# Attention, Fourier mixing and a feed-forward layer on one core: block products for all chunks, sums shared with GpSimd, new load order and schedule

## The chip, the cores and the metric

The kernel runs on one core of a Trainium2 chip. The core has engines that work beside each other, each through its own list of instructions in order: TensorE (PE, matrix products; its weight loads are listed apart, as PEld), VectorE (DVE), ScalarE (ACT), GpSimd (POOL) and SyncE (SP, which here only issues transfers). They wait for each other by semaphores. Transfers (DMAs) are issued from the queues of SP, ACT and POOL and run on 16 DMA engines.

The metric is the device time of one execution in microseconds (us); less is better. It is given as the median of several runs. A profiled execution is a run of its own: it has its own time, and its span (from the first to the last recorded instruction) is somewhat shorter than that time.

## The reference

All inputs and the output are float32. Batch B = 4, heads H = 8, sequence S = 768, head size 64, so the model width is 512; n_global = 8, n_local = 96.

```python
# attention: q, k, v (4, 8, 768, 64)
scores = scale * np.matmul(q, k.transpose(0, 1, 3, 2))
rel = pos[:, None] - pos[None, :]
is_global = pos[None, :] < int(n_global)
is_local = (rel >= 0) & (rel < int(n_local))
dist = np.where(is_global & ~is_local, float(n_local), np.abs(rel))
scores = scores - slopes[:, None, None] * dist
scores = np.where(is_global | is_local, scores, -1000000000.0)
a = softmax(scores)
x = np.matmul(a, v)            # heads side by side: (4, 768, 512)
# mixing and feed-forward
mixed = np.real(np.fft.fft(np.fft.fft(x, axis=1), axis=2))
u = x + mixed
un = (u - mean(u)) / np.sqrt(var(u) + 1e-06)
return u + np.maximum(un @ w_ch1, 0.0) @ w_ch2      # w_ch1 (512, 2048), w_ch2 (2048, 512)
```

(`softmax` stands for the three lines of the usual form, with 1e-09 added to the sum.)

## The kernel before

*The stages.* All products run on 16-bit values. For each batch b (0 to 3) there are three kinds of stage, and a fourth and fifth behind them.

- Attention. For each pair of heads, q and k are transposed; in batches 0 and 1 by TensorE (L654, with the identity `ident` as its second operand), in batches 2 and 3 by transposing transfers that SP issues (L633). Scores are then made for the band and the global keys (L731 to L751). The distances come in by a product with a table `misc` (loaded from `distm`, helper `dma_const`, L1610) in batches 0 and 1, and in batches 2 and 3 by a multiplication with masks `mk`, which ScalarE makes from a second table `distk`. ScalarE takes exponentials (L765, L768), TensorE the products with v (`pav`, L824), and VectorE divides by the sums (`norm`, L836), into a buffer X.
- Mixing. The two Fourier transforms are made by folds (sums and differences on VectorE, from `fold_0` and `fold_s`/`fold_d`; batches 1 to 3 get a mirrored copy through DRAM: `xd` is written, `xr` read by SP, and `xg` gathered by GpSimd, L889), then products with tables t1 and t2 (`y_unit`, `u_unit`, L1107 and about), a layer norm (mean, square, `rstd` on GpSimd at L1287, `un` on ScalarE or VectorE at L1271 and L1280), and a transpose of `un` to `unT`, by TensorE (L1311) or by transfer.
- First product. The 3072 rows are cut into 12 *chunks* of 2 x 128 rows, three for each batch. `ph_unit(c, jp)` makes an eighth of `relu(un @ w1)` of chunk c: 8 matmuls of 256 columns (L1341), and an evacuation with the relu on ScalarE (L1346) or VectorE (L1347), into `hT`.
- Second product, with two forms. The first CS = 2 chunks use `pg_unit(c, t, part)` (L1362): for each half t of the rows, four units of four matmuls of 512 columns (L1372), each of which needs one quarter (`part`) of w2, and one evacuation with the residual (L1383). The chunks from CS on use block products: `s_sums(c)` (L1432) makes four sums s1, s2, s4, s3 of blocks of `hT` (each 128 x 1024, VectorE), `w2_sums(i)` (L1417) makes sums of blocks of w2 once, in two halves i, and `pg_units(c)` (L1477) makes seven products of 8 matmuls of 256 columns (L1486) in place of the eight that the plain form amounts to; they are named p1, p45 (two products in one unit), p6, p7 and p32, and their results are evacuated from the banks pgA and pgD (L1504).

*The sums of w2* are made in place: `one` (L1422) reads two quarters and writes into `misc`, when the scores of batch 1 no longer need it; `rest` (L1426 to L1428) makes three more, the first of them over a block of w2 itself.

```python
def one():
    VT(W2T(1)[:, k0], W2[0][:, k1, HC:Dm], W2[0][:, k0, HC:Dm], op=ALU.subtract)
...
pl.later([("DVE", dve2(1024), one)], [("w2", 3), ("w2", 1)] + ..., 0.0, [("w2a", i)], rank=2)
pl.later([("DVE", 3 * dve2(1024), rest)], [("w2a", i), ("pgdone",)] + ..., 0.0, [("w2t", i)], rank=2)
```

`pgdone` says that the chunks below CS have read all of w2 in its first form. (`k0` and `k1` are four of the sixteen row blocks of w2 each; the half i = 0 reads quarters 0 and 2, the half i = 1 quarters 1 and 3. The list given to the planner names two of them only; the instruction itself waits for what it reads.)

*The order.* Nothing of the order on the engines comes from the program's loops. The class `Plan` holds a list for each engine, `ORDER`, written out by hand, and emits the instructions in these orders. The constants for the cost of an operation (`act`, `dve`, `pool`, the figures in the calls of `later`) tell the planner when it believes things happen; they decide in which sequence the heads of the five lists are emitted, and alter no instruction. The names in the lists:

- on PE: A0, A1, ... attention units, M0, ... mixing units, H0, ... first products (H(8c + jp) is eighth jp of chunk c), G0, ... second products;
- on the others: `H6.0` is operation 0 of unit H6 (its evacuation), and T.0, T.1, ... are the operations that belong to no PE unit, numbered as the program makes them. T.0 to T.7 are the loads of q and k of the first pair of heads, and their casts; T.8 is the identity, T.9 the distance table, T.10 the table `back`, T.26 the table t1, T.27 t2, T.35 the table `distk`, T.54 to T.57 the quarters of w1 (`wload`, L1678), T.58 to T.61 v of batch 1, T.62 to T.65 the quarters 0 to 3 of w2 (L1678), T.91 the read `xr` of batch 1. T.93 to T.98 are the fold of batch 1; T.97 is its part g1 and T.98 its part g2. The sums of w2 and of the chunks follow behind; their numbers move with the change: the two halves of `one` and `rest` are T.259 to T.262 before, and T.270 to T.273 after; the sums of the chunks begin at T.201 (chunk 2 before, chunk 0 after).

*Queues.* Most loads (q, k, v, the tables t1 and t2, w1, w2) are cast to 16 bit on their way and are issued by GpSimd one by one (`swq`), among GpSimd's computing work. The first loads (first pair of q and k, the identity, the two distance tables, `back`) and the stores are issued by SP and ACT. At the start ACT's list was `T.2 T.4 T.8 T.3 T.5` (a half of q, a half of k, the identity, two casts) and SP's `T.6 T.0 T.9 T.136 T.35 T.127 ...`: the other halves, the distance table, and, among the transposes of batch 2, `distk`. The read T.91 stood behind six of these transposes.

The functions that the change touches and what calls them:

Of the kernel before, what the change touches and what calls it, by code (L numbers as in the profile page):

```python
# [12 lines left out]
ALU = mybir.AluOpType  # L13
# [11 lines left out]
class Plan:  # L25
# [11 lines left out]
    LAT = {"ACT": 0.14, "DVE": 0.12, "POOL": 0.08}  # L37
# [84 lines left out]
    def op_go(self, eng, name, start):  # L122
# [6 lines left out]
        if eng == "POOL":  # L129
            self.ports.append((start, end, 1 if dma else 0 if outs and outs[0][0] in ("vB", "kB") else 2))  # L130
# [21 lines left out]

    SHARED = {"kB": 1, "vB": 1, "sid": 1, "f1": 0, "f2": 0, "f3": 0, "z": 0, "g0": 0, "w": 0, "s": 0, "w2a": 0, "w2t": 0, "ex": 0}
# [3 lines left out]
    def beside(self, start, cost, kind):  # L157
# [4 lines left out]
        if names:  # L162
            s = self.op_start("POOL", names[-1])
            if s is not None:
                p = self.made[names[-1]]
                ports = ports + [(max(s, start), max(s, start) + p[0]["POOL"][0], 1 if p[7] else 0 if p[3] and p[3][0][0] in ("vB", "kB") else 2)]
# [54 lines left out]
    def unit_start(self, unit):  # L221
# [7 lines left out]
        if not there:  # L229
# [1558 lines left out]
```

## Time and profile before

| | us |
|---|---|
| median of 3 runs | 248.52 (247.92 to 248.96) |
| profiled execution, its own time | 248.1 |
| its span | 246.3 |
| busy in the span: TensorE | 230.6 (94%) |
| VectorE | 193.6 (79%) |
| ScalarE | 138.6 (56%) |
| GpSimd | 114.1 (46%) |

The rows that are shown below come from these views. The page's strip cuts the span into 40 equal slices (6.16 us each) and gives a row for each engine, for the granted TensorE clock, and for the GB/s moved. A table by stretch gives the start and end of a stretch, its length, and then for each engine the busy time in it. The chain of waits goes back from the last instruction and gives start, length and what ran. The timeline gives start, duration, engine, line, operation, and `out<-in` by the names of the tiles, with the shape and the count of equal instructions put together. A group of a line gives the count and min/median/max in ns, and from when to when. The list of transfers gives name, queue, size, and the us from issue to landing. The page's list of groups gives the busy time, the mean in ns of one, and the idle time of that engine just before them with what ended it. In these names `pg` is the bank of the plain second product, `pgA` and `pgD` are those of the block products, `qk<-in_k_dram` is a load of k, `sc` a score bank, `py` that of a y product, and `u` holds the residual and, at the end, the output.

### The profile page before, as it was taken

The page shows a single profiled execution, that of the slowest core. Times are in us where ns is not written, and L with a number is a line of the kernel's source. Part 1 is how long each engine was busy: PE and PEld are TensorE (multiplying, and loading weights), DVE is VectorE, ACT ScalarE, POOL GpSimd, SP SyncE. Part 2 cuts the span into 40 slices and gives each one's busy share as a digit, 9 for nine tenths or more (in the row PEclk, how much of TensorE's full clock was granted, in tenths as well). Part 3 has the DMA queues.
Part 4 walks back from the last instruction along what each step waited for, and adds up shares of the span by engine and source line. Part 5 has one row for each costly group of instructions (what it writes and reads, how often), then busy time and mean ns, then how long its engine had stood idle before and what let it go on. Part 6 is the DMA issues. An engine that isn't in the chain of part 4 may idle for free.

```text
span 246.3 us, 7605 instructions
## 1 busy us (share of the span) xinstructions
PE 230.6 (94%) x3251; PEld 191.2 (78%) x3251; DVE 193.6 (79%) x420; ACT 138.6 (56%) x226; POOL 114.1 (46%) x162
## 2 busy tenths in 40 slices
PE   7497896999999998999999999999999999999994
PEld 2375774788668567888988888898889898888883
DVE  2389995879974669999999699899998756746483
ACT  2289687874747458677447788464443761434200
POOL 8699985978391018999139046700210230011020
PEclk9999999999999999999999999999999999999999
DMA  7999999999999999999999989221380240040212
GB/s 178 171 163 141 157 223 148 201 189 201 125 133 168 211 181 204 111 139 114 220 208 266 136 110 148 50 23 22 133 296 4 43 130 0 0 130 1 89 65 106
DMA packets 96082, 32.89 MB, mean 134 GB/s; under 512 B 84304, under 2 KB 92624, under 8 KB 96048
## 3 DMA queue, kind: packets, MB, share of 16 engines
q0 software_dynamic: 66176, 17.06, 72.7%
q1 hardware_dynamic: 26560, 12.56, 25.8%
q10 hardware_dynamic: 3312, 2.79, 3.9%
q8 instruction: 25, 0.41, 0.7%
q14 instruction: 9, 0.07, 0.1%
HBM read 31.48 MB, written 8.65 MB: 163 GB/s over the span
## 4 chain that ended last, share of the span: by engine, by line
PE 49%; DMA 21%; DVE 15%; ACT 4%; POOL 4%; SPq 3%; issue 2%; ACTq 0%; DVEq 0%; POOLq 0%
PE ph L1341 21%; PE pgD L1486 12%; PE pgA L1486 9%; DMA v<-in_v_dram 6%; DMA t<-t1m 4%; DMA ident<-idm 3%; SPq L633 3%; DMA out_dram<-u 3%; PE pav L824 2%; ACT ex L768 2%; DMA unT<-un 2%; POOL qk L554 2%; DMA xr<-xd 2%; DVE tt L836 2%; DMA qk<-in_q_dram 2%
## 5 line engine op out<-in xcount | busy, mean ns | idle before, releaser
L1341 PE MATMUL ph<-unT,w 128*128 128x256 f16 x768 | 94.4, 273 | 1.4 <-DMA unT<-un 0.7
L1341 PEld LDWEIGHTS <-w 128*128 128x128 f16 x768 | 73.7, 98 | 13.2 <-issue 1.2
L1346 ACT ACTIVATE hT<-ph 128x512 f16<-128x512 f32 x73 | 42.9, 596 | 55.1 <-PE ph L1341 53.1
L1486 PEld LDWEIGHTS <-hT 128*128 128x128 f16 x320 | 31.0, 98 | 4.3 <-issue 0.4
L1287 POOL TENSOR_SCALAR sm<-sm 128x2 f32<-128x2 f32 x12 | 3.5, 291 | 58.7 <-ACT un L1280 58.3
L765 ACT ACTIVATE er<-sc 128x1024 f16<-128x1024 f32 (+1 forms) x24 | 22.3, 951 | 11.6 <-PE sc L739 8.0
L1347 DVE TENSOR_SCALAR hT<-ph 128x512 f16<-128x512 f32 x23 | 15.7, 687 | 12.6 <-PE ph L1341 12.6
L768 ACT ACTIVATE ex<-sc 128x1024 f16<-128x1024 f32 (+1 forms) x24 | 21.6, 955 | 5.7 <-PE sc L745 5.6
L1504 DVE SCALAR_TENSOR_TENSOR u<-pgA,sm,u 128x256 f32<-128x256 f32 (+1 forms) x30 | 16.9, 568 | 5.6 <-PE pgA L1486 5.1
L1504 DVE SCALAR_TENSOR_TENSOR u<-pgD,sm,u 128x512 f32<-128x512 f32 (+1 forms) x21 | 15.1, 720 | 3.2 <-PE pgD L1486 3.0
L1357 POOL DMA_INDIRECT out_dram<-u,back x4 | 4.6, 1146 | 27.8 <-DVE rev L1142 16.3
L889 POOL DMA_INDIRECT xr<-xd,back x3 | 4.6, 1525 | 26.1 <-PE sc L739 16.6
L1120 ACT ACTIVATE zy<-py 128x1024 f16<-128x1024 f32 (+1 forms) x13 | 11.1, 857 | 8.8 <-PE py L1107 6.1
L1372 PE MATMUL pg<-w,hT 128*128 128x512 f16 x64 | 16.0, 380 | 0.0
L780 DVE TENSOR_TENSOR ex<-er,mk 128x1024 f16<-128x1024 f16 (+1 forms) x24 | 15.1, 645 | 0.7 <-ACT er L765 0.7
L1280 ACT ACTIVATE un<-un 128x512 f16<-128x512 f16 x24 | 15.0, 625 | 1.1 <-DMA unT<-un 1.1
L1271 ACT ACTIVATE un<-u,sm 128x512 f16<-128x512 f32 x19 | 13.1, 717 | 2.4 <-DVE sm L1238 1.0
L554 POOL DMA_DIRECT2D qk<-in_k_dram x16 | 13.7, 901 | 1.1 <-DMA w<-in_moe_w_ch_dram 0.7
L824 PEld LDWEIGHTS <-ex 128*128 128x128 f16 x352 | 12.6, 97 | 2.0 <-issue 1.2
L824 PE MATMUL pav<-v,ex 128*128 128x65 f16 x224 | 13.1, 193 | 0.6 <-DVE x L836 0.5
L554 POOL DMA_DIRECT2D qk<-in_q_dram x16 | 13.6, 868 | 0.0
L836 DVE TENSOR_TENSOR x<-pav,rc 128x384 f16<-128x384 f32 x24 | 12.6, 554 | 0.6
(168 smaller groups left out, 489.3 us busy)
## 6 DMA issues: line engine op xcount, KB each, us to landing
w<-in_moe_w_ch_dram POOLq DMA_DIRECT2D x8, 512.0 KB, 13.5
out_dram<-u SPq DMA_DIRECT2D x15, 256.0 KB, 2.4
v<-in_v_dram POOLq DMA_DIRECT2D x12, 192.0 KB, 7.6
qk<-in_k_dram POOLq DMA_DIRECT2D x16, 96.0 KB, 6.8
qk<-in_q_dram POOLq DMA_DIRECT2D x16, 96.0 KB, 5.3
xr<-xd SPq DMA_DIRECT2D x3, 512.0 KB, 4.7
xd<-x ACTq DMA_DIRECT2D x2, 768.0 KB, 5.6
v<-in_v_dram POOLq DMA_DIRECT2D x8, 96.0 KB, 5.4
```

The source lines that it names most:

```text
L554: nc.gpsimd.dma_start(qk16[n][:, w, :, h], src[b, h0 + h].rearrange("(i m) d -> m i d", m=P))
L765: A(mine(), cut(pa), AF.Exp, 0.0, 0.125)
L768: A(cut(expst[hp][:, :, g * 512:g * 512 + (384 if g == 2 else 512)]), cut(pa), AF.Exp, 0.0, 0.125)
L780: VT(o, mine(), m, op=ALU.mult)
L824: nc.tensor.matmul(o[:, s * 65:(s + 1) * 65], lhsT, w, start=(a == 0), stop=(a == len(ops) - 1), skip_group_check=True)
L836: VT(X[b][:, 3 * (k.start + h):3 * (k.start + h) + 3, 2 * hp * Dh:(2 * hp + 2) * Dh].rearrange("p y (h d) -> p y h d", d=Dh), pv[:, h, :, ...
L1341: nc.tensor.matmul(ph[:, a * CH:(a + 1) * CH].rearrange("p (x m) -> p x m", x=2), W1[0][:, d, jb * P:(jb + 1) * P], UNT[c][:, :, d, :], st ...
L1346: pl.later([("ACT", act(512), lambda: A(dst, ph, AF.Relu)), ("DVE", dve(512), lambda: V.tensor_scalar_max(dst, ph, 0.0))], [], e, [("h", c ...
L1347: ("DVE", dve(512), lambda: V.tensor_scalar_max(dst, ph, 0.0))],
L1372: nc.tensor.matmul(pg, HT[c][:, jb, t * P:(t + 1) * P], W2[0][:, jb, :], start=(jb == 0), stop=(jb == NJ - 1))
L1486: nc.tensor.matmul(o, lhs(j), rhs(j), start=(first and j == 0), stop=(j == NK - 1), skip_group_check=True)
L1504: V.scalar_tensor_tensor(o, x, r(t), acc, op0=ALU.mult, op1=ALU.add)
```

## The change

CS goes from 2 to 0: all 12 chunks use block products. So `pg_unit` is made for no chunk, nothing waits for `pgdone`, `w2_sums` can come before the first second product and has to come before p45 of chunk 0, and the buffer `tt` that was X of batch 1 has only one earlier user (`WTI` is 1; X of batch 1 is now the buffer `x`, which X of batch 0 also uses). For chunks above 2 a sum of `s_sums` may be put on GpSimd; the new order puts twelve there: T.221, T.220 (chunk 3), T.226 (chunk 4), T.229 (chunk 5), T.238, T.236 (chunk 6), T.242 (chunk 7), T.247, T.248 (chunk 8), T.253, T.254 (chunk 9) and T.266 (chunk 11).

The loads at the start: ACT's list becomes `T.8 T.2 T.4 T.9 T.7 T.3 T.5` and a little later `T.35`; SP's becomes `T.6 T.0 T.10 T.91 T.127 ...`. In GpSimd's list the table t1 goes ahead of the w2 quarter that stood before it, and the w2 quarters come in the order 3, 2, 1, 0; the last of them, T.62, stands behind all loads of batches 0 and 1 and behind two small ones of batch 2 (T.110 and T.103).

All five lists are new. On PE, the first products and the mixing around the start of the second products are in another sequence (the first second product, G0, comes after H13 and before H14, M18, H8 and M16; G1 is p45 of chunk 0). On VectorE, T.270 (`one`) stands between T.97 and T.98; the constants of the planner are others.

```diff
-    CS = 2
+    CS = 0
...
+def pool2(n):
+    return 0.2 + n / 450.0
...
-        def s1():
-            VT(new(0), block(1, 0), block(1, 1), op=ALU.add)
...
+        def s1(on=V):
+            on.tensor_tensor(new(0), block(1, 0), block(1, 1), op=ALU.add)
+
+        def s3(on=V):
+            on.tensor_tensor(block(1, 0), block(0, 0), block(1, 0), op=ALU.subtract)
...
         us = dve2(NK * P)
+
+        def slow(fn):
+            return [("POOL", pool2(NK * P), lambda: fn(nc.gpsimd))] if c > 2 else []
...
-        pl.later([("DVE", us, s1)], hs + sfree(0), 0.0, [("s", c, 1)], rank=1)
+        pl.later([("DVE", us, s1)] + slow(s1), hs + sfree(0), 0.0, [("s", c, 1)], rank=1)
...
-        pl.later(ways if soon else ways[:1], needs, 0.0, [tok], lat=1.0 if soon else 3.2, dma=us)
+        pl.later(ways if soon or tok == ("dk",) else ways[:1], needs, 0.0, [tok], lat=1.0 if soon else 3.2, dma=us)
...
         "PE": (
...
-            "A39 A29 M3 M9 A32 M7 A33 A40 M8 M10 A31 M6 A27 M11 M13 A44 H2 H7 A43 H4 H3 M12 A42 H0 H1 A41 H12 G4 H13 H11 G0 H6 H5 M14 G1 G5 G6 H15 G7 H14 "
+            "M3 A38 A32 A33 M7 M9 A27 A28 M8 A29 M6 A44 A31 M11 A43 M10 H2 A41 M13 A42 H0 H7 M12 H3 H1 H6 H9 H10 H5 H12 H15 H11 M15 H4 M19 H13 G0 H14 M18 "
+            "H8 M16 G1 G2 M14 M17 G3 G4 A46 H22 H19 G5 H23 H17 A47 G7 G6 H16 A45 A53 H18 H20 G8 G9 H21 A52 A51 H24 G10 M20 H26 G11 H28 H27 G12 A55 A50 "
...
         "ACT": (
-            "T.2 T.4 T.8 T.3 T.5 A1.2 A3.0 A4.0 A2.0 A8.0 A9.0 A7.0 A20.0 A18.0 A19.0 A13.0 A12.0 A14.0 A30.1 A37.0 A36.0 T.72 M0.0 T.77 M0.1 A25.1 M1.0 "
+            "T.8 T.2 T.4 T.9 T.7 T.3 T.5 A1.1 A3.0 A4.0 T.35 A2.0 A9.0 A7.0 A18.0 A20.0 A19.0 A14.0 A8.0 A13.0 A12.0 A30.1 A34.1 A35.0 T.72 T.77 M0.0 "
...
         "DVE": (
...
+            "A42.0 T.93 T.94 T.95 T.96 M13.2 T.97 T.270 T.98 T.272 T.271 T.201 T.273 M13.4 T.202 G0.0 T.99 G1.0 T.204 G2.0 T.203 M14.0 G3.0 H14.0 G4.0 "
...
         "POOL": (
...
+            "A34.0 T.26 T.60 T.27 T.59 A26.0 T.58 T.55 T.54 T.57 A25.0 T.65 T.87 T.88 T.56 T.85 T.86 T.64 T.84 T.110 T.63 T.103 T.62 T.104 T.105 T.108 "
...
+            "T.152 T.125 T.122 T.153 T.170 T.160 T.166 M17.5 T.164 T.154 T.157 T.163 T.126 T.155 T.156 T.162 T.168 T.221 T.220 M17.11 T.141 M20.5 T.226 "
...
         "SP": (
-            "T.6 T.0 T.9 T.136 T.35 T.127 T.133 T.128 G7.1 T.134 T.91 G3.1 T.10 T.137 T.130 T.100 T.131 T.101 T.102 T.176 T.182 T.177 T.34 T.185 T.183 "
+            "T.6 T.0 T.10 T.91 T.127 T.128 T.206 T.133 T.205 T.130 T.134 T.136 T.131 T.100 T.137 T.101 T.217 T.176 T.177 T.102 T.216 T.182 T.34 T.185 "
```

More of the change, by code (lines that the diff above doesn't have):

```diff
@@ L36 @@
     LANDED = {"HW": 0.55, "SW": 1.3}
-    LAT = {"ACT": 0.14, "DVE": 0.12, "POOL": 0.08}
+    LAT = {"ACT": 0.18, "DVE": 0.12, "POOL": 0.08}
     def __init__(self):
@@ L129, in op_go @@
         if eng == "POOL":
-            self.ports.append((start, end, 1 if dma else 0 if outs and outs[0][0] in ("vB", "kB") else 2))
+            self.ports.append((start, end, 1 if dma else 0 if outs and outs[0][0] in ("vB", "kB", "ts", "w1s", "s") else 2))
         if dma:
@@ L165, in beside @@
                 p = self.made[names[-1]]
-                ports = ports + [(max(s, start), max(s, start) + p[0]["POOL"][0], 1 if p[7] else 0 if p[3] and p[3][0][0] in ("vB", "kB") else 2)]
+                ports = ports + [(max(s, start), max(s, start) + p[0]["POOL"][0], 1 if p[7] else 0 if p[3] and p[3][0][0] in ("vB", "kB", "ts", "w1s", "s") else 2)]
         for a, b, dma in ports:
@@ L854, in part @@
             m = k.stop - k.start
-            pl.later([("DVE", 0.17 + 0.03 * m + m * dve(384), lambda: norm(po, k))], free(*XT[b]), e,
+            pl.later([("DVE", 0.08 + 0.03 * m + m * dve(384), lambda: norm(po, k))], free(*XT[b]), e,
                      [("x", b, hp, z) for z in range(k.start, k.stop)], CD(b, ring), ring=ring, rank=RA(b))
@@ L1274, in centre @@
         for a in range(2):
-            pl.later([("ACT", 0.62, lambda a=a: un("ACT", a)), ("DVE", 1.3 if c < 2 else 0.38, lambda a=a: un("DVE", a))],
+            pl.later([("ACT", 0.62, lambda a=a: un("ACT", a)), ("DVE", 1.3 if c < 2 else 0.55, lambda a=a: un("DVE", a))],
                      [("u", c, a)] + free("un", c), 0.0, [("un", c, a)])
@@ L1288, in rstd @@
             nc.gpsimd.tensor_tensor(r, r, mhalf, op=ALU.pow)
-        pl.later([("POOL", 0.82, rstd)], [("ss", c, 0), ("ss", c, 1)], 0.0, [("rstd", c)], rank=2)
+        pl.later([("POOL", 1.25, rstd)], [("ss", c, 0), ("ss", c, 1)], 0.0, [("rstd", c)], rank=2)
     def nt_dma(c):
```

47 lines of the change are left out of this document (23 added, 24 removed), and 59 rows, old and new, of the table ORDER.

## The prediction

> **What bounds the kernel now.** I read the busy time by stretch first, then the chain of waits, then single rows. Each row below is a stretch, its length, and the busy time (and instruction count) of TensorE (PE), its weight loads, VectorE (DVE), ScalarE (ACT) and GpSimd (POOL); then the granted clock, the DMA share and GB/s.
>
> ```profile
> 8.68:50.00 41.32, 34.94 (x900) 27.98 (x900) 34.21 (x86) 31.30 (x40) 34.73 (x54) 1.00 1.87 172
> ...
> 65.70:100.00 34.30, 33.45 (x374) 23.18 (x364) 25.10 (x55) 21.04 (x35) 16.52 (x20) 1.00 1.26 171
> 100.00:180.00 80.00, 79.46 (x1142) 69.67 (x1140) 74.91 (x154) 50.46 (x86) 39.92 (x52) 1.00 1.06 132
> 180.00:242.74 62.74, 62.70 (x588) 55.88 (x586) 43.31 (x91) 23.51 (x43) 6.39 (x10) 1.00 0.23 72
> 242.74:246.30 3.56, 0.00 (x0) 0.00 (x0) 0.48 (x1) 0.00 (x0) 0.00 (x0) 1.00 0.31 112
> ```
>
> From 65.7 us to 242.74 TensorE is idle for 1.4 us in all, and it works through a hand-written order. So the end is: the time at which some TensorE unit starts, plus the TensorE work behind it, plus a tail of 3.56 us. VectorE is the second bound: 74.91 of 80 us between 100 and 180. Only before 50 us has TensorE slack (6.4 us idle), and there the chain of waits names loads (start, length, what):
>
> ```profile
> 1.82 6.81 DMA ident<-idm
> 8.68 1.32 PE pt L654 x24
> ...
> 27.83 10.04 DMA t<-t1m
> ...
> 38.52 14.24 DMA v<-in_v_dram
> ```
>
> The first transposes wait for the identity, the first y product for the table t1, the last attention of batch 1 for v. At 172 GB/s the loads are one stream that GpSimd's queue feeds.
>
> **The change part by part.**
>
> *Start.* The identity goes from third to first on ScalarE's load queue, the distance table from SyncE's to fourth on ScalarE's.
>
> ```profile
> 1.76 0.48 SPq L1610 DMA_DIRECT2D misc<-distm  x1
> 7.18 0.52 ACT L599 ACTIVATE hT<-u 128x384 f16<-128x384 f32 x1 [2.59 <-DMA u<-in_k_dram]
> ...
> misc<-distm SPq DMA_DIRECT2D x1, 320.0 KB, 6.1
> distk<-distkm SPq DMA_DIRECT2D x1, 160.0 KB, 2.7
> ...
> 10.93 0.41 PE L731 MATMUL sc<-misc 64*64 64x512 f16 x4
> ```
>
> With the identity early, the last of the four casts (7.18 + 0.52 = 7.70) decides: 8.68 - 7.70 = 1.0 us gained. Bounds: 0.5, if that k half, now third, lands one issue (0.5) later; 1.8, if the 320 KB table no longer shares the engines with it. I take 1.0. The table now lands about where the identity did (8.6), still ahead of the first scores (10.9). The other table, distk, moves from SyncE's queue, where the transposes of batch 2 stood around it, into this stretch: 160 KB at 172 GB/s delay the GpSimd stream by 0.9 us.
>
> *Products.* Chunks 0 and 1 were 64 products of 512 columns (four rows below are four units of the order); they become 7 block products of 8 x 256 columns per chunk, as chunks 2 to 11 already are.
>
> ```profile
> 60.01 1.03 PE L1372 MATMUL pg<-w,hT 128*128 128x512 f16 x4
> 60.88 1.91 PE L1341 MATMUL ph<-unT,w 128*128 128x256 f16 x16
> ...
> 65.33 0.45 PE L1311 MATMUL ptu<-ident,un 64*64 64x64 f16 x32
> ...
> 70.92 1.03 PE L1372 MATMUL pg<-w,hT 128*128 128x512 f16 x4
> ...
> 116.81 0.87 PE pgA L1486 x8
> ```
>
> From 60.01 to 60.88 a unit of four costs 0.87 us, so a chunk costs 8 x 0.87 = 6.96; a block product costs 0.87, so 7 x 0.87 = 6.09. TensorE saves 2 x 0.87 = 1.7 us.
>
> *The new wait.* The old units took each quarter of w2 as it landed. The new second unit of chunk 0 (p45) needs all of w2, and then the w2 sums and chunk 0's first sum. When does w2 land? Issue times and times to landing of three w2 loads and the k load behind them:
>
> ```profile
> L1678 POOL DMA_DIRECT2D w<-in_moe_w_ch_dram x1: 759/759/759, 46.0 to 46.0; - x1
> DMA to landing us min/median/max: 13.0/13.0/13.0
> ...
> L1678 POOL DMA_DIRECT2D w<-in_moe_w_ch_dram x1: 742/742/742, 47.6 to 47.6; - x1
> DMA to landing us min/median/max: 13.9/13.9/13.9
> ...
> L554 POOL DMA_DIRECT2D qk<-in_k_dram x1: 822/822/822, 51.6 to 51.6; - x1
> DMA to landing us min/median/max: 13.4/13.4/13.4
> ```
>
> ```profile
> GB/s 178 171 163 141 157 223 148 201 189 201 125 133 168 211 181 204 111 139 114 220 208 266 136 110 148 50 23 22 133 296 4 43 130 0 0 130 1 89 65 106
> ```
>
> Landings at 59.0 and 61.5: 2.5 us each; the last w2 load stands between that and the k load (65.0), so it lands at about 64.0. The new GpSimd order has the same loads ahead of the last w2 load (all of batches 0 and 1, tables, weights, two small ones of batch 2); only their order differs, so 64.0 again, between 62 (the thin fourth and fifth slices of 141 and 157 GB/s below, where GpSimd made copies between its issues, filled up to 172: 2 x 6.16 us x 23 / 172 = 1.6) and 65.5 (distk, new pauses). The last is now T.62, the first quarter, and VectorE's first w2 sum (T.270) reads just that quarter.
>
> VectorE does not get there late: its last norm began at 60.47, and the new order puts A41 to A44 ahead of five first-product units (4.4 us), so about 56 to 55 even with the front as it is; the fold up to the end of g1 took 69.40 - 60.47 = 8.9.
>
> ```profile
> 60.47 1.02 DVE L836 TENSOR_TENSOR tt<-pav,rc 128x384 f16<-128x384 f32 x2
> ...
> 69.40 0.95 DVE L1077 TENSOR_TENSOR eA<-zy 128x1536 f16<-128x1536 f16 x1
> ...
> 71.20 0.74 DVE L1383 SCALAR_TENSOR_TENSOR u<-pg,sm,u 128x512 f32<-128x512 f32 x1
> ...
> 133.32 0.68 DVE L1450 TENSOR_TENSOR eg<-hT 128x1024 f16<-128x1024 f16 x1
> 133.92 0.74 DVE L1504 SCALAR_TENSOR_TENSOR u<-pgD,sm,u 128x512 f32<-128x512 f32 x1
> ```
>
> So T.270 waits at the head of VectorE's queue, at 61 to 64 us, until 64.0. Behind it stand, in order, g2 of batch 1 (71.20 - 69.40 = 1.8), a second sum, three sums, s1 of chunk 0, three sums: nine sums at 133.92 - 133.32 = 0.60 make 5.4. p45 can start at 64.0 + 5.4 + 1.8 = 71.2. TensorE meanwhile has only p1, H14, M18, H8 and M16 (4.1 us) and idles some 3 us. That is where the front's gain goes: t1 is issued ahead of the w2 quarter that stood before it (2.5 us), and the start is 1.0 earlier, but both end in this wait.
>
> *What is left at p45.* At 70.92 the old kernel had 242.74 - 70.92 = 171.8 us to go. Against that state the new one has done H8 to H10 (2.6) and the y products M15, M16, M18, M19 (24 matmuls of 256 columns, 2.6) more, and M14 (0.4) less; of chunk 0 it has six block products left (5.2) where the old had two units (1.7); chunk 1 is 0.9 cheaper. 171.8 - 2.6 - 2.6 + 0.4 + 3.5 - 0.9 = 169.6.
>
> *VectorE's load.* Eight more sums (4.8 us) and ten evacuations instead of four; twelve sums leave (7.2).
>
> ```profile
> L1383 DVE SCALAR_TENSOR_TENSOR u<-pg,sm,u 128x512 f32<-128x512 f32 x4 | 3.0, 748 | 0.2 <-PE pg L1372 0.2
> L1504 DVE SCALAR_TENSOR_TENSOR u<-pgA,sm,u 128x256 f32<-128x256 f32 x20 | 9.5, 477 | 4.5 <-PE pgA L1486 4.4
> ...
> L685 POOL COPY mk<-qkT x7: 607/614/642, 11.5 to 42.3; 128x512 f16<-128x512 f16 x7
> ...
> L1453 DVE TENSOR_TENSOR hT<-hT x10: 682/684/1107, 104.5 to 237.6; 128x1024 f16<-128x1024 f16 x10
> ```
>
> Evacuations: 6 x 748 + 4 x 477 = 6.4 against 3.0. In sum +1.0 us on VectorE, but up to 100 us it gains 8.2 and loses nothing, where it had 34.3 - 25.1 = 9.2 idle: it just fits, and without that cover the excess would fall on TensorE. A GpSimd sum isn't in the trace; a copy of 512 takes 0.61, so 1024 elements with two inputs take between 1.2 (read together) and 2.5 (one after the other); I take 2.4. The Trainium skill (GPSIMD Engine Reference, section Elementwise, side-by-side cycle accounting) gives about 2.6 cycles per element at 1.2 GHz, an estimate of 2.2 us. Two of them (T.221, T.220) stand ahead of chunk 4's rstd and the gather of batch 2 on GpSimd, which is idle for 40 of the 80 us from 100 to 180: hidden. Cost 0 to 2 us for clashes with VectorE; I take 0.5.
>
> *Moved ahead on SyncE.* The read xr of batch 1 passes the transposes of batch 2.
>
> ```profile
> 76.95 3.79 SPq L633
> ...
> 84.30 4.90 DMA xr<-xd
> ...
> PE ph L1341 <- DMA unT<-un: 0.7, 1, 0.7
> ```
>
> It took the queue at 84.3 behind that wait; earlier, TensorE's 0.7 us wait for unT may go. I take 0.5 gained, which cancels the clashes. The transposes passed serve attention of batch 2, which in the new order stands behind chunk 0's products. X of batch 1 now shares X of batch 0's buffer; its last reader (M6) already stood ahead of A44 in both orders, so no wait. The other planner constants alter no instruction by themselves.
>
> **Sum.** 71.2 + 169.6 = 240.8, + 3.56 = 244.4. The profiled execution took 248.1 for a span of 246.3, so 1.8 around it: 246.2. That execution lies 0.4 below the runs' median of 248.52; I leave 246.2.
>
> **The rivals.**
>
> *The wait on w2 doesn't decide.* If w2's first quarter is there when VectorE asks for it, at 61, the sums are done at 61 + 7.2 = 68.2 and p45 starts when TensorE gets to it, 64.0 + 4.1 = 68.1: 3.0 less, 243.2. For it: pauses in the stream could close, and the front is some 3 us earlier (start and t1), so TensorE would be there. Against: the same bytes at the same GB/s.
>
> *VectorE becomes the bound by GpSimd's sums (slower).* If a two-input VectorE instruction stands still for a whole GpSimd sum, a sum costs up to 2.4 and saves 0.6. Seven fall between 100 and 180: 7 x 1.8 = 12.6 against 80 - 74.91 = 5.1 of idle, 7.5 too much, less the 3 us that p45's own lateness and later slack cover: 246.2 + 4.5 = 250.7. It decides from a mean loss of 5.1 / 7 + 0.6 = 1.3 us per sum on. For it: L1453 once took 1107 instead of 684. Against: its median is its minimum, though GpSimd was busy half of that stretch. The Trainium skill (SBUF — State Buffer, section Who interferes with whom) states this rule: an exclusive lock, the second one fully blocked; the maximum agrees, the median hardly.
>
> *Nothing gained.* distk and pauses bring w2 at 65.5 and chunks 0 and 1, crowded on VectorE, cost another 0.5: 248.2. The start may also do nothing for the end: that is so in the forecast.
>
> **How the numbers follow.** Forecast (244.6 to 247.8) 0.50, w2 early 0.18, nothing gained 0.13, VectorE bound 0.19. Faster or slower than 248.52 by over 0.5% (1.24 us, what a measurement here can tell) means below 247.28 or above 249.76. Of the forecast 0.39 lies below and 0.11 within; w2 early is faster; of nothing gained 0.03 is faster, 0.10 same; of VectorE bound 0.18 slower, 0.01 same: 0.60, 0.22, 0.18. Range: from 243.0 (w2 early) to 250.0, which leaves out about half of the slow rival.
>
> **What would show it.** First transposes at 7.2 to 8.2 us. T.270 (line of `one`) starting after a wait on the w load, at about 64; TensorE idle about 3 us ahead of the first pgD product, which starts at 70 to 72.5. Then little TensorE idle up to an end of its work near 241. Wrong if pgD starts before 69, if the w2 sum does not wait for a load, if TensorE idles over 3 us after 75, or if two-input VectorE groups' medians rise above 0.8 us.

## The result, and the profile after

The changed kernel takes 256.56 us (median of 4 runs, 255.19 to 258.90), the kernel before beside it 248.22 (247.36 to 248.96): ratio 1.035, 95% interval 1.026 to 1.043. It is slower, where 246.2 had been forecast, and outside the range to 250.0. The profiled execution is the longest of the four runs, 2.3 us above their median: 258.9 us, span 257.1 against 246.3. Ranges hold all runs; ratios leave out runs of over 1.5% above the fastest of their kernel (that of e6 does not, see there).

The same four stretches as before, the last one up to the end of TensorE's work (now 253.49). Columns: stretch, its length, busy time of TensorE, its weight loads, VectorE, ScalarE, GpSimd, granted clock, DMA share, GB/s.

```profile
8.68:50.00 41.32, 34.49 (x812) 27.63 (x816) 28.93 (x73) 29.10 (x38) 30.88 (x46) 0.92 1.51 157
65.70:100.00 34.30, 29.84 (x354) 24.99 (x352) 26.13 (x62) 21.14 (x41) 12.60 (x18) 0.95 1.63 168
100.00:180.00 80.00, 78.43 (x1175) 67.88 (x1173) 73.78 (x145) 50.40 (x84) 49.96 (x53) 1.00 1.13 130
180.00:253.49 73.49, 71.44 (x665) 63.40 (x662) 58.37 (x109) 20.58 (x41) 21.81 (x17) 1.00 0.23 73
```

TensorE, idle for 1.4 us in all from 65.7 us on before, now loses 4.5 us between 65.7 and 100, 1.6 between 100 and 180, and 2.1 behind that. And the granted clock, 1.00 throughout before, is lower in two stretches. Where it is lower, and what TensorE waits for at 75 and at 84 us (stretches; then the timeline: start, duration, engine, line, operation, idle time before and what ended it; then the chain of waits):

```profile
12.00:19.00 7.00, 6.41 (x116) 4.87 (x119) 3.01 (x8) 2.88 (x4) 2.66 (x5) 0.51 1.47 128
87.00:91.00 4.00, 4.00 (x24) 2.94 (x23) 2.58 (x8) 2.04 (x4) 0.00 (x0) 0.57 1.19 218
```

```profile
9.41 0.52 ACT L605 ACTIVATE hT<-u 128x384 f16<-128x384 f32 x1 [3.94 <-DMA u<-in_k_dram]
9.99 1.00 PE L660 MATMUL pt<-ident,hT 128*64 128x128 f16 x18 [2.76 <-ACT hT L605]
...
69.36 0.69 DVE L1428 TENSOR_TENSOR misc<-w 128x1024 f16<-128x1024 f16 x1 [2.22 <-issue]
...
74.74 0.60 PE L1495 MATMUL pgD<-tt,hT 128*128 128x256 f16 x4
77.22 0.60 PE L1495 MATMUL pgD<-tt,hT 128*128 128x256 f16 x4 [1.88 <-DVE tt L1434]
...
86.22 0.42 PE L745 MATMUL sc<-qkT 64*32 64x128 f16 x20 [2.58 <-DMA qkT<-qk]
```

```profile
1.75 7.64 DMA u<-in_k_dram
...
58.07 11.22 DMA w<-in_moe_w_ch_dram
69.57 8.60 DMA qk<-in_k_dram
78.19 7.99 DMA qkT<-qk
86.22 0.41 PE sc L745 x8
```

The reader is to see three things. The k half that now stands third on ScalarE's queue lands at 9.39 us, so TensorE is idle for 2.76 us, and a stretch at half clock follows. The last quarter of w2 lands at 69.29; the first w2 sum starts right behind it, and the second unit of chunk 0 (p45) starts at 74.74 and stops in its middle for the other half of the sums. And the first scores of batch 2 wait 2.58 us more, for a transpose whose loads stood behind w2; another stretch at half clock follows.

What happens from 100 us on is seen around 208 us, in the timeline:

```profile
206.82 2.11 POOL L1462 TENSOR_TENSOR mk<-mk,hT 128x1024 f16<-128x1024 f16 x1 [0.98 <-DVE mk L1456]
209.01 2.45 POOL L1469 TENSOR_TENSOR mk<-hT,mk 128x1024 f16<-128x1024 f16 x1
...
207.80 1.69 DVE L1459 TENSOR_TENSOR hT<-hT 128x1024 f16<-128x1024 f16 x1
209.41 2.08 DVE L1147 COPY rev<-zy 128x2 f16<-128x2 f16 x1
...
211.67 0.68 DVE L1353 TENSOR_SCALAR hT<-ph 128x512 f16<-128x512 f32 x1
...
212.40 1.03 PE L1347 MATMUL ph<-unT,w 128*128 128x256 f16 x8 [1.76 <-DVE hT L1353]
```

Two GpSimd sums run from 206.8 to 211.5 (2.11 us, and 2.45 for the second, which began while a VectorE sum was still running). Beside them that VectorE sum takes 1.69 us instead of 0.68, and a copy of two columns takes 2.08 (0.16 in e3 below, at 200.57, where GpSimd makes no sum). The evacuation behind them starts at 211.67, and TensorE has waited 1.76 us for it. What TensorE waited for between 100 and 254 us (who, for whom: us in total, times, longest):

```profile
PE ph L1347 <- DVE hT L1353: 1.8, 1, 1.8
PE pgA L1495 <- DVE u L1513: 0.6, 1, 0.6
PE pgA L1495 <- DVE sb L1462: 0.6, 1, 0.6
```

The two waits that are left out (0.2 us each) also end with VectorE; none ends with GpSimd or with a transfer. The long one is the wait at 212.40; the other two stand at 152.16 and 126.92, behind VectorE instructions that took 2.12 and 3.95 us beside a GpSimd sum. So it is not the GpSimd sums themselves, nor loads behind them, that TensorE waits for here.

### The profile page after: what moved, and what is told of

Read it like the earlier page. It is cut to its first block, busy times and chain, and to the rows that moved or that the text cites. A ratio compares the mean times of both kernels' runs of the same rounds, so it can differ in the third digit from the quotient of the medians.

```text
span 257.1 us, 7722 instructions
## 1 busy us (share of the span) xinstructions
PE 234.9 (91%) x3299; PEld 198.8 (77%) x3299; DVE 204.1 (79%) x428; ACT 136.6 (53%) x227; POOL 135.3 (53%) x167
## 4 chain that ended last, share of the span: by engine, by line
PE 60%; DMA 15%; DVE 11%; POOL 8%; ACT 3%; issue 2%; ACTq 0%; POOLq 0%
PE ph L1347 26%; PE pgD L1495 13%; PE pgA L1495 10%; DMA qk<-in_k_dram 5%; DMA w<-in_moe_w_ch_dram 4%; DMA qkT<-qk 3%; DMA u<-in_k_dram 3%; PE sc L745 2%; PE py L1113 2%; POOL vB L803 2%; DVE u L1513 2%; PE pav L830 2%; PE pu L1200 2%; DVE x L842 2%; DVE sb L1462 2%
## 5 line engine op out<-in xcount | busy, mean ns | idle before, releaser
L1352 ACT ACTIVATE hT<-ph 128x512 f16<-128x512 f32 x71 | 42.2, 597 | 73.1 <-PE ph L1347 62.9
L1495 PEld LDWEIGHTS <-hT 128*128 128x128 f16 x384 | 37.8, 99 | 7.8 <-issue 2.7
L1513 DVE SCALAR_TENSOR_TENSOR u<-pgA,sm,u 128x256 f32<-128x256 f32 (+1 forms) x36 | 20.4, 567 | 8.3 <-PE pgA L1495 8.2
L1513 DVE SCALAR_TENSOR_TENSOR u<-pgD,sm,u 128x512 f32<-128x512 f32 (+1 forms) x25 | 18.1, 723 | 4.6 <-PE pgD L1495 4.3
L1353 DVE TENSOR_SCALAR hT<-ph 128x512 f16<-128x512 f32 x25 | 17.1, 686 | 5.1 <-PE ph L1347 4.8
L842 DVE TENSOR_TENSOR x<-pav,rc 128x384 f16<-128x384 f32 x32 | 16.7, 554 | 0.7
L1495 PE MATMUL pgD<-tt,hT 128*128 128x256 f16 x96 | 12.7, 272 | 1.9 <-DVE tt L1434 1.9
L1495 PEld LDWEIGHTS <-sb 128*128 128x128 f16 x128 | 12.3, 98 | 2.3 <-DVE sb L1462 0.7
L1459 POOL TENSOR_TENSOR hT<-hT 128x1024 f16<-128x1024 f16 x3 | 6.4, 2135 | 13.0 <-DVE mk L1456 11.9
L1495 PE MATMUL pgA<-w,hT 128*128 128x256 f16 x96 | 13.1, 282 | 0.0
```

The source lines that it names most:

```text
L842: VT(X[b][:, 3 * (k.start + h):3 * (k.start + h) + 3, 2 * hp * Dh:(2 * hp + 2) * Dh].rearrange("p y (h d) -> p y h d", d=Dh), pv[:, h, :, ...
L1352: pl.later([("ACT", act(512), lambda: A(dst, ph, AF.Relu)), ("DVE", dve(512), lambda: V.tensor_scalar_max(dst, ph, 0.0))], [], e, [("h", c ...
L1353: ("DVE", dve(512), lambda: V.tensor_scalar_max(dst, ph, 0.0))],
L1495: nc.tensor.matmul(o, lhs(j), rhs(j), start=(first and j == 0), stop=(j == NK - 1), skip_group_check=True)
L1513: V.scalar_tensor_tensor(o, x, r(t), acc, op0=ALU.mult, op1=ALU.add)
```

## The experiments

Twelve kernels, each timed beside the kernel before. Theory "start": the late k half, through clock, GpSimd's queue and late loads, makes the two waits at 75 and 84 us. Theory "lock": VectorE stands still during GpSimd's sums. Rivals: the waits lie in the place of the new products, whatever the start; and VectorE cannot carry the sums itself. Medians and ranges, ratio to the kernel before with its interval:

| kernel | us | ratio |
|---|---|---|
| changed kernel | 256.56 (255.2 to 258.9) | 1.035 [1.026, 1.043] |
| e1 its start put back | 253.61 (252.6 to 254.3) | 1.021 [1.014, 1.028] |
| e2 more warm-up matmuls | 255.18 (254.6 to 256.5) | 1.030 [1.023, 1.037] |
| e3 its sums on VectorE | 250.98 (248.8 to 252.4) | 1.011 [1.006, 1.016] |
| e4 one copy off GpSimd | 257.54 (255.6 to 258.9) | 1.036 [1.027, 1.045] |
| e5 w2 loads ahead of copies | 255.69 (254.0 to 256.7) | 1.029 [1.023, 1.035] |
| e6 scores of batch 2 later | 259.21 (255.1 to 260.8) | 1.046 [1.040, 1.053] |
| e7 start and sums | 250.67 (248.9 to 253.8) | 1.007 [1.003, 1.011] |
| e8 e1, e3, e5 and e6 | 251.93 (249.8 to 254.5) | 1.014 [1.008, 1.019] |
| e9 kernel before, sums on GpSimd | 254.19 (253.2 to 262.6) | 1.023 [1.017, 1.028] |
| e10 kernel before, new start | 249.06 (247.5 to 253.1) | 1.005 [1.001, 1.008] |
| e11 start in full, and sums | 249.37 (248.1 to 251.6) | 1.005 [1.002, 1.009] |
| e12 four of the sums on VectorE | 251.07 (250.2 to 256.5) | 1.013 [1.008, 1.018] |

Stretches at half clock differ from run to run of one kernel and make a part of the wide ranges: the mean granted clock of single runs lies between 0.960 and 1.000, and of e3, for one, the runs at 0.991 or more took 248.8 to 250.2 and those at 0.986 or less 251.8 to 252.4. They do not make all of it: the longest run of e2 (256.54) had a clock of 1.000 and its shortest (254.56) 0.992. Where the rest comes from is open.

**e1: the loads at the start put back.**

```diff
 "ACT": "T.8 T.2 T.4 T.9 T.7 T.3 T.5 ..."  ->  "T.2 T.4 T.8 T.7 T.3 T.5 ..."
 "SP":  "T.6 T.0 T.10 T.91 ..."            ->  "T.6 T.0 T.9 T.10 T.91 ..."
```

> The changed kernel with the loads at the start put back: ScalarE's queue issues q, k and then the identity, SyncE's queue the distance table third (distk and everything else stay as changed). Theory 'start': the k half that now stands third on ScalarE's queue landed at 9.39 us instead of about 7.2, TensorE stood idle for 2.76 us, its granted clock was 0.5 from 12.6 to 19 us, GpSimd waited 4.28 us for a copy of those transposes with its loads queued behind it, and so the last w2 load (69.3 us) and the q and k loads of batch 2 (up to 78.2 us) came late. It expects: first transposes done by 10, granted clock 1.00 up to 70 us, last w2 landing at 64 to 66.5, TensorE idle between 75 and 90 us below 2 us instead of 4.5, and 249 to 252 us in all. Rival 'place': the products of chunk 0 wait for all of w2 and the scores of batch 2 for loads behind it, whatever the start; it expects the waits after 75 us to stay within 1 us of 4.5 and the time above 254.

It took 253.61, between the two. The k half was cast at 6.57, no stretch at half clock came before the end, but the last w2 quarter still landed at 68.5 and TensorE was idle for 1.4 us between 70 and 75 and 1.7 between 75 and 90. So in this run the old start goes with a full clock, but the landing of w2 is not explained by it. The four runs had clocks of 0.993 to 1.000, those of the changed kernel 0.980 to 0.993. (The start was not back in full: a cast stood behind the products with the identity, on VectorE, until 8.87.)

**e2: thirty warm-up matmuls instead of fifteen** (`PZ = 15` to `PZ = 30`).

> The changed kernel with 30 instead of 15 of the matmuls on zeros that TensorE runs before its first real work, so that it is busy to about 9.8 us and not idle from 7.23 to 9.99. Nothing else moves; the k half still lands at about 9.4. Theory 'start' in the form that the clock is most of it: the granted clock stays 1.00 from 12 to 19 us, the second transposes end about 0.7 us and the copy on GpSimd some 2 us earlier, the last w2 quarter lands by 67.5, and the time is 252.5 to 254.5. Rival: the late k half is the cost and the clock adds little in a stretch in which TensorE is not the bound; it expects a time within 1 us of 256.5.

The clock, in two stretches of this run:

```profile
12.00:19.00 7.00, 5.26 (x164) 4.16 (x164) 3.95 (x11) 4.63 (x6) 2.74 (x5) 1.00 1.48 129
26.00:30.00 4.00, 3.55 (x61) 3.26 (x60) 3.08 (x7) 1.45 (x1) 3.83 (x7) 0.58 1.59 162
```

12 to 19 us now has the full clock; a stretch at half clock came at 26 instead. 255.18 lies just outside the rival's band and 0.7 short of the theory's: the clock at the start alone is not most of the loss.

**e3: the twelve sums on VectorE.** Each is put into VectorE's list where GpSimd would have started it.

```diff
 "POOL": "... T.168 T.221 T.220 M17.11 T.141 M20.5 T.226 ..."  ->  "... T.168 M17.11 T.141 M20.5 ..."
 "DVE":  "... A59.0 A49.1 G16.0 A60.0 G17.0 ..."  ->  "... A59.0 T.221 A49.1 G16.0 A60.0 T.220 G17.0 ..."
```

> The changed kernel with its twelve GpSimd sums moved to VectorE, each at the place in VectorE's order where GpSimd would have started it. Theory 'lock': a VectorE instruction that reads and writes 16-bit values in SBUF alone stands still while GpSimd makes a sum (2.1 us): seven such instructions lost about 10 us together in the profile of the changed kernel, and TensorE waited for some of them. It expects no VectorE sum above 1.2 us, TensorE idle between 100 and 242 us down from 3.6 to at most 2.0, and 253 to 255 us. Rival 'load': VectorE was the scarce engine, 12 sums cost it 7.2 us that it does not have, and the time is 256.5 or more.

250.98: 5.6 less, more than the theory asked for, and no VectorE sum of `hT` took more than 0.7 us. TensorE between 100 and 220 us, in e3:

```profile
100.00:140.00 40.00, 40.00 (x576) 34.95 (x574) 36.29 (x72) 24.46 (x43) 24.25 (x30) 1.00 1.58 183
140.00:180.00 40.00, 40.00 (x584) 34.83 (x582) 38.02 (x88) 24.83 (x43) 10.39 (x16) 1.00 0.50 98
180.00:220.00 40.00, 40.00 (x385) 36.03 (x383) 33.87 (x76) 11.45 (x21) 3.00 (x4) 1.00 0.20 52
```

and in the changed kernel:

```profile
100.00:140.00 40.00, 39.05 (x585) 33.78 (x583) 35.43 (x62) 24.32 (x42) 30.66 (x33) 1.00 1.70 165
140.00:180.00 40.00, 39.38 (x592) 34.10 (x591) 38.34 (x84) 26.08 (x43) 19.30 (x21) 1.00 0.57 94
180.00:220.00 40.00, 38.24 (x359) 34.22 (x357) 34.04 (x69) 12.46 (x23) 11.27 (x7) 1.00 0.28 86
```

Idle 3.33 us there becomes none. VectorE makes nine sums more there and is hardly busier (108.18 us against 107.81): with the sums on GpSimd it had spent that time standing still, and standing still counts as busy. Rival "load" is out. The idle time is 3.3 of the 5.6 us. The rest cannot be placed by these two profiles: they also differ ahead of 100 us, where the edit changes nothing (e3's has no half clock before its end, and TensorE is idle for 2.1 us between 70 and 90 instead of 4.5).

**e4: one copy, A5.0, from GpSimd to VectorE** (behind A5.1 in VectorE's list).

> The changed kernel with one copy of keys (A5.0, 0.9 us) moved from GpSimd to VectorE, right behind the copy out of PSUM that it reads. GpSimd's queue then has nothing that waits for TensorE ahead of the loads of v of the first pairs. Theory 'start': GpSimd issues no load from 12.4 to 17.6 us because of this copy, and the stream runs dry at 17 to 19 us; without it the last w2 quarter lands 2 to 4 us earlier (65 to 67.5) and the time is 253 to 255, though the clock at the start stays 0.5. Rival: the gap is filled later anyway (the loads are held back by something else), the last w2 quarter lands within 1 us of 69.3, and the time within 1 us of 256.5.

The last w2 quarter landed at 67.2, 2.1 us earlier as expected, but the time, 257.54, did not fall. p45 started 1.7 us earlier (73.02), but the first scores of batch 2 then waited 3.66 us instead of 2.58. The stream of loads has the gap, and the gap is not what the end hangs on. (Its profile has two stretches at half clock, as the changed kernel's.)

**e5: w2's loads ahead of copies.**

```diff
 "POOL": "... T.65 T.87 T.88 T.56 T.85 T.86 T.64 T.84 T.110 T.63 T.103 T.62 T.104 ..."
     ->  "... T.65 T.87 T.88 T.64 T.63 T.62 T.56 T.86 T.84 T.110 T.103 T.104 ..."
 "DVE":  "... A44.0 M11.0 ..."  ->  "... A44.0 T.85 M11.0 ..."
```

> The changed kernel with the loads of three w2 quarters (T.64, T.63, T.62) moved ahead of a w1 quarter and of two of the copies of v (T.85, T.86) that GpSimd makes between its issues; T.85 goes to VectorE. Theory 'copies': the last w2 load was late because GpSimd copied v for 8 us (45.4 to 54.1) in the middle of its list, not because the stream is slow; issued some 5 us earlier it lands 3 to 5 us earlier (64 to 66.5), and the second product of chunk 0 starts by 72. Then theory 'series' says: the time that this frees is taken by the next wait, the scores of batch 2 (their transposes landed at 86.2 us), whose own loads do not move, so the time falls by 1.5 us at most (255 to 256.5). Rival: the wait for w2 was the one that set the end, and the whole 2 to 4 us come out (252.5 to 254.5).

The last w2 quarter was issued at 50.45 instead of 58.07 and landed at 65.7 instead of 69.3, and the idle time inside p45 was gone. p45 did not start earlier (76.21): TensorE itself came there no sooner. Its front had lost time before, 1.45 us of short waits from 50.8 to 54.2 and then half clock to 57.6 (1.7 us); whether the copies, now later, caused that is not shown. 255.69 is what "series" said, and the scores of batch 2 still waited (1.04 us).

**e6: the first scores of batch 2 behind five ready units** (A46 behind H17 in TensorE's and ScalarE's lists).

> The changed kernel with the first scores of batch 2 (A46) put behind the five units that followed them (H22, H19, G5, H23, H17; 4.4 us of TensorE work that needs nothing of batch 2), on ScalarE's list likewise. Theory 'late transposes': TensorE's idle 2.58 us at 83.6 to 86.2, and the stretch at clock 0.5 behind it (87.3 to 90.7, 1.7 us lost) both go: TensorE idle between 80 and 92 us under 0.5, clock 1.00 there, 252.5 to 254.5 us in all. Rival: the work is only put in another order, VectorE's and ScalarE's work behind the scores comes 4 us later and stops TensorE there instead: time within 1 us of 256.5.

No gain shows. Its four runs took 255.05 and 258.13 at clocks of 0.993 and 0.987 (mean 256.6, as the changed kernel) and 260.29 and 260.83 at 0.980 and 0.971; the ratio in the table holds the longer ones, and by the first two it would be about 1.03. In its profile, the run of 255.05, the scores no longer wait for the transpose, but the next scores wait 1.81 us for ScalarE's exponentials (at 88.22), as the rival had it; no half clock followed. The order alone moves the wait and does not take it away; what it is worth at an equal clock is not settled by these runs.

**e7: e1 and e3 together; e8: e1, e3, e5 and e6 together.**

> The changed kernel with both the loads at the start put back (as in e1) and the twelve sums on VectorE (as in e3). e1 alone took 2.9 us off, e3 alone 5.6 us, but the runs of e3 lie in two bands (248.8 to 250.2 and 251.8 to 252.4), which theory 'start' takes for starts without and with a stretch at half clock, since the k half lands at chance times about the edge. It expects one band, 247.5 to 250. Rival: the effects are the same microseconds twice and the bands have another cause; it expects 250.5 to 252.5, in two bands again.

> The edits of e1, e3, e5 and e6 together: old loads at the start, sums on VectorE, w2 loads ahead of copies, first scores of batch 2 later. If the start, the sums and the two waits are the whole loss, what is left of the change is the 1.7 us of TensorE work that block products save and a front as before: 245 to 247.5 us, not slower than the kernel before. If block products for chunks 0 and 1 have a cost of their own (VectorE's 8 more sums, the later first second product), 249 to 251 us.

e7 took 250.67, e8 251.93. The start adds nothing to e3 (at clocks of 0.997 or more e7 takes 249.05 to 251.25, e3 248.84 to 249.54), and e7 still shows half clock from 10 to 17 us: the old order of loads, with one cast still late, does not prevent it. Theory "start" falls as a cause of microseconds that add to the sums'. How much of e1's 2.9 us was clock is not settled: its runs had the higher clocks, but the one at 0.993 (254.15) is also 2.5 below the changed kernel's at 0.993 (256.61). e8 shows no gain from the edits of the two waits either.

**e9: the lock alone, on the kernel before.** Its order is unchanged but for twelve sums of the same chunks and kinds, put on GpSimd where VectorE made them (`s1` to `s4` get the argument `on`, as in the change).

> The kernel before, with nothing of the change but this: the twelve sums of the same chunks and kinds are made by GpSimd, each where VectorE made it in time. Theory 'lock': VectorE's instructions on 16-bit values in SBUF stand still during the sums, and TensorE waits for some; 3 to 6 us slower than the kernel before (251 to 254.5), with VectorE sums or copies of over 1.2 us in the trace. Rival 'load': VectorE has 74.9 of 80 us busy between 100 and 180, and 7.2 us less work on it makes room: 247 to 249.

254.19: 6.3 us slower by the medians of all runs, 5.6 by the ratio. The largest stall, in its timeline:

```profile
147.91 4.64 DVE L784 TENSOR_TENSOR ex<-er,mk 128x768 f16<-128x768 f16 x2
...
147.70 2.15 POOL L528 DMA_DIRECT2D v<-in_v_dram  x2
149.85 2.14 POOL L1454 TENSOR_TENSOR eg<-hT 128x1024 f16<-128x1024 f16 x1
...
152.65 0.81 ACT L769 ACTIVATE er<-sc 128x768 f16<-128x768 f32 x1 [2.76 <-DVE ex L784]
...
153.51 0.53 PE L743 MATMUL sc<-qkT 64*32 64x128 f16 x20 [2.38 <-ACT er L769]
153.97 1.89 PE L1493 MATMUL pgD<-tt,hT 128*128 128x256 f16 x8
```

The second of two multiplications by masks stands still while GpSimd issues two loads and then makes its sum, and ends at 152.55, 0.56 us after the sum. ScalarE waits for it, and TensorE waits 2.38 us for ScalarE, and its products behind that take 1.89 instead of 1.04: half clock again, from 153.6 to about 157. So a stall costs its idle time, and sometimes 1.7 us of clock on top.

**e10: the new start alone, on the kernel before.**

```diff
 "ACT": "T.2 T.4 T.8 T.3 T.5 ..."  ->  "T.8 T.2 T.4 T.9 T.3 T.5 ..."
 "SP":  "T.6 T.0 T.9 T.136 ..."    ->  "T.6 T.0 T.136 ..."
```

> The kernel before with the new loads at the start alone: identity first on ScalarE's queue, then q, k and the distance table; distk stays on SyncE. As the prediction had it, the last cast would start by 7.7 and the first transposes be done 1.0 us earlier. Theory 'third place': the k half lands at 8.5 to 9.4, as in the five traces with this order, the first transposes end 0.2 to 1.0 us later than in the kernel before, and the time is 248.5 to 250.5, with more runs below clock 0.995 than the kernel before has. Rival (the prediction): 0.5 to 1 us faster, 247 to 248.

```profile
8.59 0.52 ACT L599 ACTIVATE hT<-u 128x384 f16<-128x384 f32 x1 [2.93 <-DMA u<-in_k_dram]
```

The cast of the third load starts at 8.59, against 7.18 in the kernel before; the time is 249.06, 1.2 us more than the 247.85 beside it. The third place costs what the early identity wins, and a little more. (Whether it is the place, or the 320 KB table that now follows on the same queue, is not separated.)

**e11: sums on VectorE and the start back in full** (e7, and the casts T.7 and T.1 first in VectorE's list).

> The changed kernel with the twelve sums on VectorE and the start put back in full: the loads as in e1 and e7, and also the two casts ahead of the products with the identity on VectorE (in e1 and e7 one cast stood behind these and waited until 8.9 to 9.6 us). What is left of the change is block products for chunks 0 and 1 and the new order. Theory: first transposes done by 10.1, as before; the waits for w2 and for the transposes of batch 2 remain, so in runs at clock 0.997 or more it takes 248 to 249.5, as e3 and e7 do, since the front's gain ends in these waits. Rival: the front carries through to the end and the kernel takes 246.5 to 247.8 in such runs, less than the kernel before.

```profile
72.45 0.60 PE L1495 MATMUL pgD<-tt,hT 128*128 128x256 f16 x4
74.40 0.60 PE L1495 MATMUL pgD<-tt,hT 128*128 128x256 f16 x4 [1.34 <-DVE tt L1434]
...
81.86 0.42 PE L745 MATMUL sc<-qkT 64*32 64x128 f16 x20 [1.04 <-DMA qkT<-qk]
```

249.37. The first transposes start at 8.74, as before, and the two waits are there all the same, shorter: TensorE is idle for 2.77 us between 70 and 90, where the kernel before has none. That is what is left of the change without its sums and its start: ratio 1.005, slower by 1.5 us by the medians instead of faster by 1.7. Its median is 1.6 us below e3's, but at clocks of 0.997 or more the two are alike (248.1 to 250.1, and 248.8 to 249.5): what the start in full seems to win is fewer runs at a low clock.

**e12: four of the twelve sums on VectorE** (T.221, T.226, T.247, T.248).

> The changed kernel with four of the twelve GpSimd sums on VectorE: those of chunk 3 at 124.2 us, chunk 4 at 149.6 and chunk 8 at 206.8 and 209.0, beside which a VectorE instruction that TensorE needed next took 2.1 to 3.9 us. Eight sums stay on GpSimd. Theory 'lock on the path': only stalls ahead of something that TensorE waits for cost time; TensorE idle between 100 and 220 us falls from 3.3 us to at most 0.7, and in runs of equal clock it takes 3 to 4.5 us less than the changed kernel, 251 to 253 us. Rival: each sum costs the same, so four of twelve give back a third of e3's 5.6 us: 254 to 255.

251.07: 5.5 us less, as much as all twelve gave. Its profile is of the longest of its runs (256.5), with half clock early on, but from 100 to 220 us its clock was 1.00 and TensorE was idle for 0.41 us. Eight sums stayed on GpSimd and cost nothing that shows. So the price is not the same for each sum: by this run it is paid where a stalled VectorE instruction stands ahead of something that TensorE needs next.

## Why the prediction was wrong, point by point

The forecast had the end of TensorE's work at 240.8; the profile has 253.49, 12.7 us later. By the prediction's own terms: p45 started 3.5 late (74.74 for 71.2); its stop in the middle cost 1.9, the scores of batch 2 2.6, the half clock behind them 1.7 (3.4 us at 0.5), the idle time from 100 to 220 us 3.3. That makes 13.0. This is the account of the profiled execution; the median of the runs misses the forecast by 10.4 us (256.56 for 246.2).

- **What bounds the kernel**: held. The tail was 3.6 (253.49 to 257.1), and from p45 to the end, 178.75 us less the 9.5 of stalls and clock behind its start, there were 169.3 us of TensorE work for the forecast 169.6.
- **Clashes on VectorE, "Cost 0 to 2 us ... I take 0.5"**: this step failed, and by the runs it is the largest term: e3 and e9 put it at about 6 us (5.6, and 5.6 to 6.3), of which 3.3 can be read as idle time in the changed kernel's profile. The mechanism was on record as the slower rival; its length of a sum was close (2.4 for 2.1), and its VectorE load held (it just fits, by e3). What was wrong was the reading that spoke against it, that L1453's median is its minimum "though GpSimd was busy half of that stretch". What GpSimd was busy with there, in the kernel before from 100 to 180 us (busy us and mean ns of one):

```profile
L524 POOL DMA_DIRECT2D v<-in_v_dram x6 | 6.2, 1037 | 0.0
L554 POOL DMA_DIRECT2D qk<-in_q_dram x7 | 6.0, 863 | 0.0
L797 POOL COPY vB<-v 32x528 f16<-32x528 f16 x7 | 5.5, 779 | 0.4
L554 POOL DMA_DIRECT2D qk<-in_k_dram x6 | 5.0, 835 | 0.0
L795 POOL COPY vB<-v 128x528 f16<-128x528 f16 x7 | 4.8, 689 | 1.3 <-DMA v<-in_v_dram 1.3
L1288 POOL TENSOR_TENSOR sm<-sm,mhalf 128x2 f32<-128x2 f32 x5 | 4.1, 817 | 0.4
```

  17.2 of 39.9 us were issues of loads, 10.3 copies with one input, and the only two-input instructions had two columns. The trace of before held nothing like the sums and could not speak against the lock, nor for it: L1453's one slow instance (at 104.50) ran beside the issue of three loads (104.15 to 106.64). The rival's price was 4.5 us over the forecast, not far off, but it was worked out as 1.8 us for each of seven sums less a cover, and e12 shows that four sums in bad places can make nearly all of it. Its test, medians above 0.8 us, could not have shown it: the medians stayed at 0.68, and the time sits in some seven instructions of 1 to 4 us.
- **The start, 1.0 us earlier**: failed. "the last of the four casts (7.18 + 0.52 = 7.70) decides" took the k half for one issue later at most. Third on its queue it was cast at 8.5 to 9.6 in the profiles with the new order (9.41 in that of the changed kernel), and the transposes ended 1.0 us later than before (10.99 for 9.99). e10: 1.2 us slower (interval 0.3 to 2.1), not 0.5 to 1 faster. That the front hardly reaches the end was right (e7 and e11 against e3).
- **w2 at 64.0, bounds 62 to 65.5**: failed; 69.3. The step "the new GpSimd order has the same loads ahead of the last w2 load ...; only their order differs" counted loads and left out what GpSimd does between them:

```profile
45.43 0.64 POOL L801 COPY vB<-v 128x528 f16<-128x528 f16 x1
...
52.88 1.28 POOL L803 COPY vB<-v 16x528 f16<-16x528 f16 x2
54.11 0.74 POOL L1687 DMA_DIRECT2D w<-in_moe_w_ch_dram  x1
...
58.07 0.78 POOL L1687 DMA_DIRECT2D w<-in_moe_w_ch_dram  x1
```

  Four sets of copies of v (and a w1 load) now stand between the first of the w2 loads and the rest, so the last is issued at 58.07, against 50.24 before. e5 moved the loads ahead and had w2 at 65.7.
- **The wait for all of w2 and for its sums**: right, with its place and its work. The first sum starts at the landing, after VectorE has waited; p45 then waits for sums in two parts, 5.4 and 7.9 us behind it, where one point at 7.2 was forecast. But the forecast's 3 us of idle TensorE ahead of p45 were not there in this profile:

```profile
65.70:74.74 9.04, 9.04 (x86) 8.10 (x84) 6.68 (x14) 6.89 (x16) 5.02 (x8) 1.00 1.82 218
```

  TensorE worked without a gap up to p45, and came to it at 74.74 where the forecast had 68.1 for its front; the first sums were ready at 74.5. So front and sums were late together (the front has the late start and the half clock from 12 to 19 us ahead of it), and an earlier w2 alone does not bring TensorE to p45 sooner (e5).
- **"The transposes passed serve attention of batch 2, which in the new order stands behind chunk 0's products", cost nothing**: failed. Its loads stand behind w2 on GpSimd's queue, and the wait costs 2.6 us and then clock. With e5 and e6 each of the two waits could be moved, and the time did not fall; e11 leaves both at 2.4 us together.
- **The clock**: no term for it. The profile of before had 1.00 up to its end.

The slower side had a chance of 0.18 and ended at 250.0; two unknowns that both pointed up (the lock and the new wait) were priced as alternatives, and in the profile they add.

What stays open: whether block products for chunks 0 and 1 can pay here. From e11's 2.8 us of idle time one can estimate that w2 and the loads of batch 2 would have to come some 3 us earlier, with nothing else later; no run tests that. No kernel that was run is faster than the one before.

## What to carry to other kernels

Before work is moved to GpSimd, see what it did beside VectorE in the trace at hand: load issues and tiny operations are no evidence on a sum of 1024 columns, and the cost falls where a VectorE instruction that stays in SBUF stands ahead of what TensorE needs next, so choose the places and not the count. When a load is moved in a queue, count all the work of the engine that issues it, not the loads alone. And a short wait of TensorE can cost up to its length again in clock: 1.7 us behind 2.4 and 2.6 us here.

## What the runs showed of the hardware

- While GpSimd makes a two-input sum of 1024 columns (2.11 us), VectorE instructions that stay in SBUF stand still until it ends, even a copy of two columns (2.08 us): in the changed kernel eight of them started within one of the twelve sums, and each ended with that sum or up to 0.6 us behind it; those that read PSUM go on: the evacuation at 207.19, from the last row below, took its usual 0.69 us in the middle of the sum that began at 206.82. The longest stalls (3.95 us in the changed kernel, rows below; over 4 in e9) began in GpSimd's issue of two loads with the sum directly behind. The issue of loads alone did not do it: in e3 a VectorE sum took its 0.68 us at 117.14, in the middle of two issues from 116.73 on. The Trainium skill (SBUF — State Buffer, section Who interferes with whom) states an exclusive lock for the whole instruction against VectorE's fast modes or two SBUF inputs; these rows agree.

```profile
122.50 1.65 POOL L560 DMA_DIRECT2D qk<-in_q_dram  x2
122.92 3.95 DVE L1462 TENSOR_TENSOR sb<-eg,hT 128x1024 f16<-128x1024 f16 x1
124.15 2.16 POOL L1459 TENSOR_TENSOR hT<-hT 128x1024 f16<-128x1024 f16 x1
...
207.19 0.69 DVE L1353 TENSOR_SCALAR hT<-ph 128x512 f16<-128x512 f32 x1 [0.46 <-PE ph L1347]
```

- Half clock came after single idle times of 1.8 to 2.8 us (1.81 in e5, 1.90 in e6, 2.38 in e9, 2.58 and 2.76 in the changed kernel), and once after none above 0.72 (e5 at 54.2: TensorE was busy for 1.95 of the 3.40 us before it). It did not come after others of 2.3 to 2.5 (2.32 in the kernel before, 2.49 in e11, 2.50 in e8). It lasted 6.8 and 3.4 us in the changed kernel, and about 10 once in e12. The Trainium skill (TensorE: Matmul & The Clock Gate, section Part 1: The HAM clock gate (the "warmup" mystery)) has a free-running window of about 3.4 us that decides on the clock; the lengths agree, and with such a window equal idle times may cost the clock or not.
